# First-layer operands as float16 pairs instead of float32r pairs in a fused attention and two-layer kernel

## The chip, the core and the metric

The kernel runs on one core of a Trainium2 chip. The metric is the device time of one execution in microseconds (us). A core has a matrix engine (TensorE, called PE in the profile, with its weight loads as PEld), a vector engine (DVE), an activation engine (ACT), a general engine (POOL) and a queue engine (SP) that issues transfers. Each takes its own instructions in program order.

## The reference

Three stages follow one another; all tensors are float32 except the four weight matrices of the layers, which come as float64.

```python
kv_pool = kv.reshape(B, H // 4, 4, W // 4, 4, C).mean(axis=(2, 4))   # 384 x 32 -> 96 x 8 = 768 keys, C = 128
k = v = kv_pool.reshape(B, -1, C) @ w_sr
s = (q @ k.transpose(0, 2, 1)) / np.sqrt(C)                          # 12288 queries
a = np.exp(s - s.max(-1, keepdims=True)); a /= a.sum(-1, keepdims=True) + 1e-09
x = a @ v
h = x @ moe_w_in                                                     # 128 -> 2048
x2 = (h * np.clip(h + 3.0, 0.0, 6.0) / 6.0) @ moe_w_out              # 2048 -> 128
h2 = x2 @ moe2_w_in
g = np.where(h2 >= 1, h2, np.where(h2 <= -1, 0.0, (h2 + 1) ** 2 / 4))
out = g @ moe2_w_out
```

## The kernel before

A product of two float32 matrices is made of parts. Each operand is split into a high part and a low part (the remainder), and three matmuls are summed in PSUM: high by high, high by low, low by high. In attention's second product the parts are float16; everywhere else (queries and keys, both layers) they are float32r, a 32-bit type of the matrix engine.

The 12288 queries are 24 blocks of 512. The hidden width of 2048 is 8 pairs of 128-wide pieces, so a block has 8 **slots**, 192 in all. In slot T the function `slot` (L589) issues, for layer 1: `m_in` (L458 on: 6 matmuls of 512 columns into two PSUM tiles `h`), `relu1` on ACT, `mul1` on DVE, `hi_lo` (ACT makes the high part, POOL subtracts to get the low part) and, a slot later, `m_out` (L467: 6 matmuls of 512 columns that add to `acc`). Layer 2 runs 11 slots behind layer 1 in the same slots, with `clip2` and `max2` on DVE and `sq2` on ACT in place of relu and product. Four PSUM tiles `h` go round: two for layer 1 and two for layer 2. So a slot has 24 matmuls of 512 columns, 12 of each layer. Layer 2 alone is left in the last 11 slots.

The attention of later blocks is spread over the slots: in a block of slots there are four score steps (`s_mm`: 6 float32r matmuls of 384 columns, a maximum on DVE, an exponential on ACT), four tails (`s_tail_a`, `s_tail_b`: L423 and L428 on DVE, then a transposing DMA) and two value steps (`av`: 18 float16 matmuls of 256 columns, then L448 on ACT and L449 on DVE, which scale and split `x`).

Ahead of the slots a hand-written order, the string PROLOGUE, gives every step of the start: pooling of the 12 key loads (`k`, `g`, `t`), keys and values (`p`, `z`, `y`), scores and softmax of block 0 (`s`, `S`, `n`, `N`, `e`, `a`, `b`), the scale of V (`vm`, `vr`, `vs`), its parts (`vh`, `vl`), the two value products of block 0 (`x0`, `x1`), and parts of the weight conversion. `j5.1` is stage 1 of weight job 5. There are 16 weight jobs (a quarter of one matrix each, 512 KB of float64), and every job has four stages: two ACT instructions (stage 0), two on DVE and one on POOL (stage 1), one on DVE (stage 2), and a high and a low part (stage 3). What the prologue doesn't do is done in the slots that CONV_AT lists. The string LOADS gives the order of loads; a load is issued when a staging buffer is free. Staging buffers are borrowed from the tiles of the slots (`t1`, `h1`, `l1`, `g2`, `h2`, `l2`, two each) and two of their own (`wst`).

## Time and profile before

| what | value |
|---|---|
| median of 3 runs | 1358.77 us (1357.54 to 1359.09) |
| the profiled execution | 1357.68 us |
| its span, first to last instruction | 1355.9 us |
| PE busy | 1316.6 us, 97% |
| PEld busy | 1074.1 us, 79% |
| DVE busy | 1160.5 us, 86% |
| POOL busy | 1072.3 us, 79% |
| ACT busy | 1035.9 us, 76% |
| mean granted TensorE clock | 0.990 of full speed |

Busy shares are means over the whole span. Matmuls overlap in the records, so the time of one matmul in a stream is read from the distance between starts and not from its own length. An engine is the limit of a stretch where it has no idle time there and the others have.

### The profile page before, as it was taken

What the parts mean: (1) busy time and instruction counts of PE and PEld (TensorE: products, weight loads), DVE (VectorE), ACT (ScalarE), POOL (GpSimd) and SP (SyncE); (2) the same over time, 40 slices, a digit from 0 to 9 for tenths busy, and PEclk for the clock granted to TensorE, in tenths of its full rate; (3) what the DMA queues carried; (4) which work ended last, traced back from release to release, by engine and by line L of the source; (5) the groups of instructions that cost most, each with busy time, mean ns of one, the idle gap of its engine ahead of it and who ended that gap; (6) DMA issues with size and microseconds to landing.
All of it is one profiled execution on the core that took longest, in us unless ns stands there. A gap on an engine that the chain in (4) does not pass through costs nothing.

```text
span 1355.9 us, 18468 instructions
## 1 busy us (share of the span) xinstructions
PE 1316.6 (97%) x6247; PEld 1074.1 (79%) x6247; DVE 1160.5 (86%) x1817; ACT 1035.9 (76%) x1917; POOL 1072.3 (79%) x825
## 2 busy tenths in 40 slices
PE   8578999999999999999999999999999999999998
PEld 7466788888888888888888888888888888888876
DVE  3888978888998988988889989889888889898677
ACT  3777888877777777787778777777877787777776
POOL 2488998888887887887888878878878888787886
PEclk9788999999999999999999999999999999999999
DMA  9632121221221212221212212222222122121001
GB/s 327 156 66 59 39 52 36 39 51 31 44 41 35 51 32 44 40 44 31 51 32 43 44 31 52 32 43 40 44 35 48 32 43 38 30 44 24 8 9 16
DMA packets 260783, 66.28 MB, mean 49 GB/s; under 512 B 252368, under 2 KB 256592, under 8 KB 260688
## 3 DMA queue, kind: packets, MB, share of 16 engines
q1 hardware_dynamic: 259456, 62.94, 24.0%
q10 hardware_dynamic: 1232, 2.16, 0.4%
q8 instruction: 49, 0.80, 0.2%
q14 instruction: 46, 0.38, 0.1%
HBM read 21.04 MB, written 6.29 MB: 20 GB/s over the span
## 4 chain that ended last, share of the span: by engine, by line
PE 87%; DVE 4%; ACT 1%; POOL 1%; issue 1%; DMA 0%; ACTq 0%; DVEq 0%; POOLq 0%
PE acc L480 38%; PE h L464 37%; PE s L371 6%; PE s L443 6%; POOL l L540 1%; DVE t L511 1%; DVE a L428 1%; DVE wa L173 0%; DVE nm L382 0%; ACT t L505 0%; DVE wa L175 0%; DMA wst<-in_moe_w_out_dram 0%; ACT a L421 0%; DVE g L518 0%; ACT h L539 0%
## 5 line engine op out<-in xcount | busy, mean ns | idle before, releaser
L540 POOL TENSOR_TENSOR l<-g,h 128x512 fp32r<-128x512 f32 x382 | 507.0, 1349 | 222.6 <-ACT h L539 175.2
L540 POOL TENSOR_TENSOR l<-t,h 128x512 fp32r<-128x512 f32 x382 | 496.0, 1321 | 9.6 <-ACT h L539 7.2
L505 ACT ACTIVATE t<-h 128x512 f32<-128x512 f32 x384 | 228.2, 599 | 219.1 <-PE h L464 202.7
L511 DVE SCALAR_TENSOR_TENSOR t<-t,h 128x512 f32<-128x512 f32 x384 | 249.7, 683 | 129.4 <-ACT t L505 129.3
L528 DVE TENSOR_TENSOR g<-h,g 128x512 f32<-128x512 f32 x384 | 245.9, 682 | 13.5 <-ACT g L524 6.7
L539 ACT CAST h<-t 128x512 fp32r<-128x512 f32 x384 | 225.2, 620 | 34.9 <-DVE t L511 29.6
L518 DVE TENSOR_SCALAR g<-h 128x512 f32<-128x512 f32 x384 | 246.1, 682 | 1.1 <-POOL l L540 0.6
L524 ACT ACTIVATE g<-g 128x512 f32<-128x512 f32 x384 | 228.2, 629 | 1.9 <-DVE g L518 1.9
L539 ACT CAST h<-g 128x512 fp32r<-128x512 f32 x384 | 217.6, 617 | 4.3 <-DVE g L528 4.0
L464 PE MATMUL h<-xh,wi0h 128*128 128x512 f32 x384 | 153.5, 400 | 4.1 <-ACT xh L448 2.7
L480 PE MATMUL acc<-h,wo0h 128*128 128x512 f32 x384 | 157.1, 409 | 0.0
L480 PE MATMUL acc<-l,wo0h 128*128 128x512 f32 x384 | 154.7, 403 | 2.1 <-POOL l L540 2.0
L464 PE MATMUL h<-x2h,wi1h 128*128 128x512 f32 x384 | 152.8, 398 | 2.4 <-DVE g L528 2.2
L480 PE MATMUL acc<-h,wo0l 128*128 128x512 f32 x384 | 153.2, 399 | 0.0
L464 PE MATMUL h<-xh,wi0l 128*128 128x512 f32 x384 | 152.8, 398 | 0.0
L480 PE MATMUL acc<-h,wo1l 128*128 128x512 f32 x384 | 152.8, 398 | 0.0
L464 PE MATMUL h<-xl,wi0h 128*128 128x512 f32 x384 | 152.6, 398 | 0.0
L464 PE MATMUL h<-x2l,wi1h 128*128 128x512 f32 x384 | 152.6, 397 | 0.0
L480 PE MATMUL acc<-h,wo1h 128*128 128x512 f32 x384 | 152.0, 396 | 0.5 <-DVE o L496 0.4
L480 PE MATMUL acc<-l,wo1h 128*128 128x512 f32 x384 | 152.1, 396 | 0.0
L464 PE MATMUL h<-x2h,wi1l 128*128 128x512 f32 x384 | 151.6, 395 | 0.0
L428 DVE SCALAR_TENSOR_TENSOR a<-e,rc,a 128x768 f16<-128x768 f32 x96 | 122.7, 1278 | 2.8
(139 smaller groups left out, 2142.6 us busy)
## 6 DMA issues: line engine op xcount, KB each, us to landing
q<-in_q_dram SPq DMA_DIRECT2D x96, 64.0 KB, 2.4
out_dram<-o SPq DMA_DIRECT2D x96, 64.0 KB, 2.0
h<-in_kv_dram SPq DMA_DIRECT2D x4, 512.0 KB, 9.5
l<-in_moe_w_in_dram SPq DMA_DIRECT2D x3, 512.0 KB, 8.7
at<-a SPq DMA_TRANSPOSE x96, 3.6
...
```

Of the source, the lines that this page charges most:

```text
L371: nc.tensor.matmul(ps[h], l[:, js], r[:, ks], start=(n == 0), stop=(n == 2))
L428: nc.vector.scalar_tensor_tensor(out=a[:, 1], in0=e, scalar=rc, in1=a[:, 0], op0=ALU.mult, op1=ALU.subtract)
L443: nc.tensor.matmul(ps, l[:, k, :], r[:, k, :], start=(n == 0), stop=(n == 3 * KC - 1))
L464: nc.tensor.matmul(ps, l[:, ws], r, start=(n == 0), stop=(n == 2))
L480: nc.tensor.matmul(acc[m], l[:, ws], r[:, k, :], start=(c == 0 and i == 0), stop=(c == NPAIR - 1 and i == 5))
L505: nc.scalar.activation(out=g_t[0, s][:, k], in_=h_t[0, s, k], func=ACTF.Relu, scale=1.0 / 6.0, bias=0.5)
L511: nc.vector.scalar_tensor_tensor(out=g, in0=g, scalar=1.0, in1=h_t.pop((0, s, k)), op0=ALU.min, op1=ALU.mult)
L518: nc.vector.tensor_scalar(out=g_t[1, s][:, k], in0=h_t[1, s, k], scalar1=1.0, scalar2=-1.0, op0=ALU.min, op1=ALU.max)
L524: nc.scalar.activation(out=g, in_=g, func=ACTF.Square, scale=0.5, bias=0.5)
L528: nc.vector.tensor_tensor(out=g, in0=h_t.pop((1, s, k)), in1=g, op=ALU.max)
L539: nc.scalar.copy(out=hi[:, k], in_=g[:, k])
L540: eng.tensor_tensor(out=lo[:, k], in0=g[:, k], in1=f32(hi[:, k]), op=ALU.subtract)
```

## The change

The layer-1 operands (`x`, the matrices `moe_w_in` and `moe_w_out`, and the activations between them) get float16 parts. Float16 has a narrow range, so they are scaled: `x` stays in units of V's power-of-two scale, and each weight matrix is multiplied by a factor taken from its largest magnitude; `relu1`, `mul1` and the step that makes `x2` take the factors back out, with the per-partition scalars `h_sc` and `o_sc` (`relu1` had a constant before). The largest magnitude needs all four quarters of a matrix before the first of them is converted: 8 new steps `m0` to `m7` (a maximum over a quarter, on DVE), two chains `ia ib ic` and `oa ob oc` (maximum, PE transpose, nine small DVE instructions on one partition, PE broadcast, one DVE product) and `hs`. Loads and prologue steps are put in another order, the staging pool `wst` gets 6 buffers in place of 2, and `h1`, `l1` (now half as large) no longer serve as staging nor, in the last 11 slots, as buffers of layer 2.

```diff
-LOADS = "w k0 k1 w k4 k6 k2 k5 k3 w q0 k8 k7 k9 k10 k11 w w w w w q1 w w w w w w q2 w w"
+LOADS = "w k0 k1 w w w k4 k6 k2 k5 k3 q0 k8 k7 k9 k10 k11 w w w w q1 w w w w w q2 w w w"
-j0.0 j0.1 k0 j1.0 k1 j0.2 k2 k3 g2 k4 g3 j1.1 t1 k5 j2.0 j0.3 p1 q0 k6 z1 t2 j2.1 p2 t0
-j1.2 j1.3 k7 j2.2 p0 z0 k8 t3 z2 k9 p3 s0 y3 k10 z3 y2 k11 n0 t4 y1 s2 t5 p4 p5
-n2 j3.0 z4 z5 y5 s1 y4 n1 j4.0 y0 S2 S0 j3.1 N0 j2.3 S1 N1 s3 n3 N2 e0 e1 vm S3
-a0 j3.2 vr b0 e2 a1 j4.1 N3 e3 a2 b1 vs a3 vh b2 b3 vl j5.0 j3.3 j5.1 q1 j4.2 j5.2 j6.0 x0
-j4.3 x1 j6.1 j5.3
+m0 k0 m2 k1 m4 k2 m6 ia k3 g2 ib k4 ic g3 j0.0 j2.0 t1 k5 j0.1 p1 q0 k6 z1 t2 j2.1 p2 t0
+j0.2 j4.0 k7 j0.3 j2.2 p0 z0 k8 t3 z2 k9 j2.3 j4.1 p3 s0 y3 k10 z3 y2 k11 n0 t4 y1 s2 t5 p4 p5
+n2 j4.2 z4 z5 y5 s1 y4 n1 m1 y0 S2 S0 m3 N0 j4.3 m5 S1 N1 m7 oa s3 n3 N2 e0 ob e1 vm S3
+a0 oc vr j1.0 b0 e2 a1 j1.1 N3 e3 a2 b1 j3.0 vs a3 vh b2 b3 vl hs j1.2 j3.1 q1 j1.3 j3.2 j5.0 x0
+j3.3 x1 j5.1
+N_ST = 6
+W_DT = (FP16, F32R)
+H_SC = 2.0 ** -22
-CONV_AT = (0, 1, 4, 6, 7, 8, 10, 12, 14)
+CONV_AT = (0, 1, 4, 6, 7, 8, 10, 12, 13, 14)
-    w_in = [[const.tile([128, DFF], F32R, name=f"wi{m}{p}") for p in "hl"] for m in range(2)]
+    w_in = [[const.tile([128, DFF], W_DT[m], name=f"wi{m}{p}") for p in "hl"] for m in range(2)]
...
-        tags = (("t1", "h1", "l1", "g2", "h2", "l2"), ("g2", "h2", "l2"), ("wst",))[late]
+        tags = (("t1", "g2", "h2", "l2", "wst"), ("g2", "h2", "l2", "wst"), ("wst",))[late]
...
+    def w_max(job):
+        m, which, i = job
+        n = 2 * m + (which == "out")
+        nc.vector.tensor_reduce(out=mw[n][:, i:i + 1], in_=wst[job][0][:, :, 1].bitcast(FP32),
+                                axis=AX.X, op=ALU.max, apply_absolute_value=True)
+    def w_top(n, ps):
+        nc.vector.tensor_reduce(out=mw[n][:, 0:1], in_=mw[n], axis=AX.X, op=ALU.max)
+        nc.tensor.transpose(ps[0:1, :], mw[n][:, 0:1], ident)
+    def w_row(n, ps, bc):
+        nc.vector.tensor_reduce(out=top[:, 4:5], in_=ps[0:1, :], axis=AX.X, op=ALU.max)
...
+        nc.tensor.matmul(bc, ones, top[:, 0:4])
+    def w_scales(n, bc):
+        nc.vector.tensor_tensor(out=w_sc[n], in0=bc, in1=w_k, op=ALU.mult)
...
-            x_t[b] = [x_p.tile([128, BLK], F32R, tag=f"x{p}", name=f"x{p}") for p in "hl"]
+            x_t[b] = [x_p.tile([128, BLK], FP16, tag=f"x{p}", name=f"x{p}") for p in "hl"]
...
-            out=g_t[0, s][:, k], in_=h_t[0, s, k], func=ACTF.Relu, scale=1.0 / 6.0, bias=0.5
+            out=g_t[0, s][:, k], in_=h_t[0, s, k], func=ACTF.Relu, scale=h_sc, bias=0.5 * H_SC
-            out=g, in0=g, scalar=1.0, in1=h_t.pop((0, s, k)), op0=ALU.min, op1=ALU.mult
+            out=g, in0=g, scalar=H_SC, in1=h_t.pop((0, s, k)), op0=ALU.min, op1=ALU.mult
...
-        n = 1 if m == 0 or (s >= NS - O2 and s % 2) else 2
-        hi = hl_p.tile([128, 2, 512], F32R, tag=f"h{n}", name=f"h{n}")
-        lo = hl_p.tile([128, 2, 512], F32R, tag=f"l{n}", name=f"l{n}")
+        n = m + 1
+        dt = W_DT[m]
+        hi = hl_p.tile([128, 2, 512], dt, tag=f"h{n}", name=f"h{n}")
+        lo = hl_p.tile([128, 2, 512], dt, tag=f"l{n}", name=f"l{n}")
...
+    load_order = [0, 2, 4, 6, 1, 3, 5, 7] + list(range(8, 16))
```

## Rows read from the trace of the kernel before

**Rows 1.** Busy time of each engine by stage of the span, granted clock behind it.
```profile
0.00:56.50 56.50, 37.40 (x259) 31.43 (x259) 31.57 (x71) 26.60 (x59) 18.13 (x19) 0.88 0.87 257
56.50:170.00 113.50, 99.05 (x440) 76.80 (x441) 103.39 (x149) 92.81 (x170) 96.79 (x67) 0.94 0.31 66
170.00:1315.00 1145.00, 1144.58 (x5401) 937.86 (x5400) 992.54 (x1547) 888.60 (x1643) 929.08 (x718) 1.00 0.22 38
```
**Rows 2.** The chain that ended last, shares of the span by line.
```profile
PE acc L480 38%; PE h L464 37%; PE s L371 6%; PE s L443 6%; POOL l L540 1%; DVE t L511 1%; DVE a L428 1%; DVE wa L173 0%; DVE nm L382 0%; ACT t L505 0%; DVE wa L175 0%; DMA wst<-in_moe_w_out_dram 0%; ACT a L421 0%; DVE g L518 0%; ACT h L539 0%
```
**Rows 3.** Timeline of PE: first and last matmul of three unbroken runs.
```profile
696.37 0.39 PE L443 MATMUL s<-at,vh 128*128 128x256 f16 x2
698.23 0.27 PE L443 MATMUL s<-at,vl 128*128 128x256 f16 x1
...
701.15 0.40 PE L464 MATMUL h<-xh,wi0h 128*128 128x512 f32 x1
703.73 0.39 PE L464 MATMUL h<-x2h,wi1l 128*128 128x512 f32 x1
703.96 0.34 PE L371 MATMUL s<-kTh,qh 128*128 128x384 f32 x1
704.84 0.34 PE L371 MATMUL s<-kTh,ql 128*128 128x384 f32 x1
```
**Rows 4.** One block of eight slots: PE, PEld, DVE, ACT, POOL busy.
```profile
595.60:648.74 53.14, 53.14 (x254) 43.62 (x253) 46.99 (x73) 41.14 (x76) 42.61 (x33) 1.00 0.22 40
```
**Rows 5.** The same stretch as the second of rows 1, ACT's `relu1` alone.
```profile
56.50:170.00 113.50, 19.84 (x36) 0.94 0.31 66
```
**Rows 6.** Timeline of PE and DVE in that block, around its tightest place.
```profile
596.46 1.33 DVE L511 SCALAR_TENSOR_TENSOR t<-t,h 128x512 f32<-128x512 f32 x2 [2.32 <-ACT t L505]
603.22 1.93 DVE L428 SCALAR_TENSOR_TENSOR a<-e,rc,a 128x768 f16<-128x768 f32 x1
607.65 1.29 DVE L528 TENSOR_TENSOR g<-h,g 128x512 f32<-128x512 f32 x2
608.57 0.39 PE L464 MATMUL h<-x2h,wi1h 128*128 128x512 f32 x1
```
**Rows 7.** Groups of ACT that read PSUM, by shape.
```profile
L448 ACT ACTIVATE xh<-s,csc 128x256 fp32r<-128x256 f32 x43 | 19.7, 458 | 0.0
L487 ACT CAST x2h<-acc 128x512 fp32r<-128x512 f32 x24 | 13.8, 576 | 0.0
L278 ACT ACTIVATE kTh<-h 128x128 fp32r<-128x128 f32 x6 | 1.6, 280 | 0.2 <-PE h L272 0.2
```
**Rows 8.** POOL groups: layer 1's subtraction and the conversion's addition; busy, mean ns, idle before.
```profile
L540 POOL TENSOR_TENSOR l<-t,h 128x512 fp32r<-128x512 f32 x382 | 496.0, 1321 | 9.6 <-ACT h L539 7.2 <-issue 2.4
L177 POOL TENSOR_TENSOR wa<-wa,wr 128x512 int32<-128x512 int32 x16 | 21.5, 1347 | 32.7 <-DVE wa L175 31.5 <-DVE su L415 1.2
```
**Rows 9.** Groups of DVE: maxima over 384 and 768 columns.
```profile
L382 DVE TENSOR_REDUCE nm<-s 128x1 f32<-128x768 f32 x94 | 89.7, 955 | 0.3 <-PE s L371 0.3
L376 DVE TENSOR_REDUCE n<-h 128x1 f32<-128x384 f32 x4 | 2.2, 550 | 2.3 <-PE h L371 2.3
```
**Rows 10.** Timeline of the start: PE, then DVE.
```profile
13.99 2.78 PE L246 MATMUL h<-h,pool_m 128*32 128x128 f32 x16
49.38 0.58 PE L443 MATMUL h<-at,vh 128*128 128x256 f16 x2 [8.13 <-DMA at<-a]
...
43.71 1.18 DVE L428 SCALAR_TENSOR_TENSOR a<-e,rc,a 128x768 f16<-128x768 f32 x1
44.81 0.15 DVE L303 TENSOR_SCALAR mxa<-acc 128x1 f32<-128x1 f32 x1
44.99 0.15 DVE L304 TENSOR_SCALAR mxa<-mxa 128x1 uint32<-128x1 uint32 x1
```
**Rows 11.** Timeline of the end: PE and ACT in one slot of layer 2.
```profile
1327.41 0.40 PE L480 MATMUL acc<-h,wo1l 128*128 128x512 f32 x1
1328.17 1.16 ACT L539 CAST h<-g 128x512 fp32r<-128x512 f32 x2 [0.21 <-DVE g L528]
```

More of the change, by code (lines that the diff above doesn't have):

```diff
@@ L154, in w_load @@
         return True
+    mw = [const.tile([128, 4], FP32, name=f"mw{n}") for n in range(4)]
+    wm = {}
+    def w_max(job):
[6 more added lines that the diff above has]
+        nc.tensor.transpose(ps[0:1, :], mw[n][:, 0:1], ident)
@@ L160, in w_stage0 @@
+    def w_scales(n, bc):
+        nc.vector.tensor_tensor(out=w_sc[n], in0=bc, in1=w_k, op=ALU.mult)
     def w_stage0(job):
         t = wst[job][0]
+        m, which, i = job
+        half = W_DT[m] == FP16
+        sc = w_sc[2 * m + (which == "out")]
         a = wk_p.tile([128, WP], U32, tag="wa", name="wa")
         r = wk_p.tile([128, WP], I32, tag="wr", name="wr")
-        nc.scalar.activation(out=a.bitcast(FP32), in_=t[:, :, 1].bitcast(FP32), func=ACTF.Abs)
+        nc.scalar.activation(out=a.bitcast(FP32), in_=t[:, :, 1].bitcast(FP32), func=ACTF.Abs,
+                             scale=sc[:, 0:1] if half else 1.0)
@@ L165, in w_stage0 @@
         low = t.rearrange("p a b -> p (a b)").bitcast(U8).rearrange("p (a b) -> p a b", b=8)
-        nc.scalar.activation(
-            out=r, in_=low[:, :, 3], func=ACTF.Copy, scale=1.0 / 32.0, bias=1.0 / 64.0
-        )
+        if half:
+            nc.scalar.activation(out=r.bitcast(FP32), in_=low[:, :, 3], func=ACTF.Identity,
+                                 scale=sc[:, 2:3], bias=sc[:, 1:2])
+        else:
+            nc.scalar.activation(
+                out=r, in_=low[:, :, 3], func=ACTF.Copy, scale=1.0 / 32.0, bias=1.0 / 64.0
+            )
@@ L181, in w_stage2 @@
         hi32 = wst[job][0][:, :, 1]
-        nc.vector.scalar_tensor_tensor(out=hi32, in0=hi32, scalar=0xC0000000, in1=a,
+        keep = 0x80000000 if W_DT[job[0]] == FP16 else 0xC0000000
+        nc.vector.scalar_tensor_tensor(out=hi32, in0=hi32, scalar=keep, in1=a,
                                        op0=ALU.bitwise_and, op1=ALU.bitwise_or)
@@ L194, in w_stage3 @@
         eng = nc.vector if job in LO_DVE else nc.gpsimd
[L195 removed]
+        h = hi[:, sl] if W_DT[m] == FP16 else f32(hi[:, sl])
+        eng.tensor_tensor(out=lo[:, sl], in0=w, in1=h, op=ALU.subtract)
     def conv_stage(n, st):
@@ L668, in tile_attn_moe_moe2 @@
                 steps[f"j{n}.{st}"] = lambda n=n, st=st: conv_stage(n, st)
+        for n in range(8):
+            steps[f"m{n}"] = lambda n=n: w_max(w_jobs[n])
+        for n, k in enumerate("io"):
+            steps[k + "a"] = lambda n=n: w_top(n, row)
+            steps[k + "b"] = lambda n=n: w_row(n, row, bc[n])
+            steps[k + "c"] = lambda n=n: w_scales(n, bc[n])
         for j in range(4):
```

73 lines of the change are left out of this document (53 added, 20 removed).

## The prediction, made before the changed kernel was run

> **What bounds the kernel now.** I read the busy times by stage first. From 170 to 1315 us PE is busy for 1144.58 of 1145.00 us, while DVE, POOL and ACT have 13 to 22% of that stretch idle [rows 1]. The chain of waits says the same: 75% of the span is two PE lines, the first and second products of the layers (L464, L480), and another 12% attention's products [rows 2]. So in the middle a shorter matmul is a shorter kernel, until another engine takes over. Before 170 us it is otherwise: the first 56.5 us are the start, and of the next 113.5 us PE is idle for 14.5 us, in which DVE (103.39 us busy), POOL and ACT set the pace [rows 1].
>
> Second, the timeline, for what a matmul costs. Starts, not lengths, count. Twelve float32r matmuls of 512 columns go from 701.15 to 703.73 in 11 steps: 0.2345 us each. Six of 384 columns take 5 steps of 0.176. Eighteen float16 ones of 256 columns take 17 steps of 0.1094 [rows 3]. Per column that is 0.458 ns, 0.458 ns and 0.427 ns. The granted clock is 1.00 there [rows 1], and a column at 2.4 GHz is 0.417 ns. So a float32r column costs the same extra at both widths, 10%, which looks like a rate; what the float16 matmul has above its columns is 2.7 ns if it is a fixed part, or 2.6% if it is a rate. The three kinds follow one another without a gap, so a change of type between neighbours costs nothing visible.
>
> Third, one block of eight slots: 53.14 us, all PE; DVE 46.99, POOL 42.61, ACT 41.14 [rows 4]. DVE is the next bound, at 88%.
>
> **The matmuls.** Layer 1 has 12 matmuls of 512 columns in each of 192 slots: 2304. In float16 one takes 0.2160 us (fixed part: 213.3 + 2.7 ns) to 0.2188 us (rate: twice 0.1094) [rows 3]; I take 0.2165, nearer to the fixed part, because the granted clock leaves little else. The saving is 18.0 ns each, 41.4 us in all, between 36.2 and 42.6. A block would fall to 53.14 - 96 x 0.018 = 51.4 us, still above DVE's 46.99 [rows 4].
>
> The Trainium skill (TensorE: Matmul & The Clock Gate, "Back-to-back issue gap") gives the warm distance as N/2.4 plus about 2.5 ns, with no dependence on type; that would be 215.8 ns for 512 columns. The float32r rows do not follow it, they are 18.7 ns above; the float16 rows do within 0.3 ns. By it the saving would be an estimated 43.1 us, and my sum would end 1.7 us lower.
>
> **Where the saving does not arrive: the first slots.** ACT has 36 `relu1` before 170 us, so 18 slots lie in the stretch that DVE, POOL and ACT pace [rows 5]. They hold 18 x 12 x 0.018 = 3.9 us of the saving. PE waits there in some slots only; I give back 2.0, between 0 and 3.9.
>
> **Where it does not arrive: a tight place in each block.** In the block at 595.60 DVE works without a pause from 596.46 on, through a whole tail. The second product of layer 2 in the block's third slot starts at 608.57, and the `max2` that frees its PSUM tile runs as a pair of 1.29 us from 607.65, so its first half ends near 608.30: 0.27 us to spare [rows 6]. Thirty layer-1 matmuls stand on PE from the block's first product to this place, which makes PE 0.54 us earlier; DVE's run begins after three of them, so it starts only 0.05 us earlier and takes as long as before. So 0.27 - 0.54 + 0.05 = -0.22: PE waits 0.22 us once a block. To this comes the new scalar of `relu1`, on which DVE's run begins. An ACT instruction from PSUM takes 280 ns for 128 columns and 576 for 512 with a constant scale, so some 380 for 256; with a per-partition scale it takes 458 [rows 7]: 0.08 us more, if the whole difference is the scalar (0 if it is not). That makes 0.30 us; in 22 blocks 6.6 us. Both ends: nothing, if a tail's L428, 1.93 us here [rows 6], takes the 1.18 us that it has at 43.71 with POOL idle more of the time [rows 10]; 22 us, if the moved POOL work lengthens it by another 0.7 us. ACT itself gets 16 x 0.08 = 1.3 us a block and stays at 42.4 of 51.4 [rows 4].
>
> **POOL's subtraction.** It now reads a float32 and a float16 tile and writes float16. No row has POOL with float16; with float32 it takes 1321 ns and the conversion's integer addition 1347 [rows 8], so I take no change. The lower bound is half of it, which would help nothing that bounds; the upper end is the third rival.
>
> **The start.** It gains eight maxima over 512 columns. Over 384 and 768 columns they take 550 and 955 ns [rows 9]; I take 0.68 us. Four of them and the chain `ia ib ic` come among the key loads. The pooling of `k4`, at 13.99 now, stands on PE behind the broadcast of `ib` [rows 10], which waits for `m6`, that is for four weight quarters that are now loaded ahead of `k4`, then for a transpose and nine small dependent DVE instructions, 0.19 us apart (44.81 to 44.99 [rows 10]), 1.7 us. PE pools almost without a pause after it, so what it loses stays: I take 2.5 us, between 0 (the loads come as early as before) and 4.5 (chain of some 3 us and one more quarter). In the scores of block 0, the other four maxima (2.7 us), the chain's DVE part (2.0) and `hs` (three small instructions, 0.5, behind the path) stand on DVE ahead of `b1`; three conversion pieces leave the stretch and two come in, 0.85 less. `b1` ends at 44.9 and its transposed tile is what the first value product waits for at 49.38 [rows 10]. About 0.4 us falls into DVE's gaps: 3.5 us later, between 0.5 and 5.5. One more weight job is left to the slots, with two POOL instructions of 1.3 us and four of DVE; in the paced stretch I count 1.5 us, between 0 (six own staging buffers also end a wait for a load) and 3.
>
> **The end.** Layer 2 loses its second pair of buffers in the last 11 slots. ACT's high part at 1328.17 overwrites a tile that was read last by a product that started at 1327.41 or before, so it would find it free already [rows 11]. Later slots run one slot more behind, where the wait is real but ends ahead of the next use: 0.5 us, between 0 and 2.
>
> **Sum.** -41.4 + 2.0 + 6.6 + 2.5 + 3.5 + 1.5 + 0.5 = -24.8 on the profiled execution's own 1357.7: 1332.9. That execution is 1.1 below the median of the runs shown, so in terms of the median 1334.0.
>
> **Rivals.** *The gain arrives nearly whole* (chance 0.18). The tight place gives way because DVE's L428 is quicker when POOL moves, and the start costs 3 us: -42 + 1 + 3 = 1320. For it: DVE has 6 us of a block idle [rows 4]. Against it: the idle time is not where the tight place is.
>
> *DVE becomes a second bound* (0.13). Each block loses 1 us rather than 0.30, and the start all of its upper bounds, 11 us: -40 + 3 + 22 + 11 + 1 = 1355. For it: DVE would be at 91% of a block and its L428 doubles beside POOL. Against: only one place of a block has under half a microsecond to spare.
>
> *Slower: POOL is slower with float16* (0.06). A block has 16 subtractions of layer 1 among 42.61 us of POOL [rows 4]. It passes DVE's and PE's new pace when one takes 1321 + (51.4 - 42.6) / 16 = 1.87 us, and the kernel is slower than before from (53.1 - 42.6) / 16 more, 1.98 us, on, before the start is counted. At twice the time, 2.64 us, a block takes 63.7: 23 x 10.6 + 10 = 1601 us. For it: no row shows the type on POOL. Against: integer and float take alike there [rows 8], as if elements were counted. The Trainium skill (GPSIMD Engine Reference, "Elementwise — side-by-side cycle accounting") counts two-input work by elements, 2.6 cycles for each, and not by bytes; by that this rival falls away, but no row here has the type.
>
> *No gain: the extra 21 ns of a float32r matmul belong to long products and not to the type* (0.03). Then only the costs are left: 1357.7 + 2 + 6 = 1366. Against: 384 and 512 columns cost the same per column, and 256 less [rows 3].
>
> **How the numbers follow.** The forecast has 0.60. Its own range, from the bounds taken singly, is 1325 to 1345. The range reaches to the first and into the second rival: 1319 to 1352. Left out are about a third of the first rival, 0.06, two fifths of the second, 0.05, and the last two, 0.09: 0.20. A measurement of this kernel tells about 0.2%, 2.7 us, from no change. Faster than that: forecast, first rival and nearly all of the second, 0.90. Within: 0.02, the edge of the second. Slower: most of the last two, 0.08.
>
> **What would show it.** Right: layer-1 matmuls 0.216 to 0.219 us apart, layer 2 unchanged at 0.2345; a block of about 51.7 us with one PE wait of some 0.3 us for `max2` (L528's line); the first product of layer 1 near 62.5 us in place of 56.56; `relu1` some 0.08 us longer; POOL's layer-1 subtraction at 1.3 us. Wrong: a cadence that stays, PE waits for POOL in every slot, several DVE waits in a block, or a start that costs over 10 us.

## The result, and the profile after

The changed kernel takes 1343.12 us (median of 4, 1342.1 to 1343.68), the kernel before on the same chip 1358.22 us (median of 4, 1357.54 to 1359.09): a ratio of 0.9888 with a 95% interval of 0.987 to 0.9905. The forecast was 1334.0 us, its range 1319 to 1352. So the kernel is faster, as forecast, but by 15.1 us (1.1%) and not by 24.8. The profiled execution has a span of 1341.9 us, 14.0 less than the 1355.9 of before.

Where the 14.0 come from is read best from one event that every slot has: the start of its first `relu1` in the trace. This table is made from those starts (us), for all kernels of this study; the experiments follow below (e10 and e13 are experiment 10, e12 is 11, e14 is 9, the others have their number).

```
                     slot 0  slot 3  slot 9  slot 16  slot 18  slot 191     end
before                 57.8    75.4   110.0    156.4    170.7    1310.3  1355.9
after                  69.8    87.0   121.0    168.2    190.0    1295.3  1341.9
e1_job14_early         70.0    87.3   123.6    168.9    183.1    1288.6  1335.1
e2_ib_before_k3        68.7    86.0   120.0    167.2    189.0    1294.4  1340.9
e3_chain_no_wait       63.2    80.5   114.4    161.7    183.0    1288.3  1334.8
e4_const_scales        60.5    77.8   111.7    158.9    180.4    1286.0  1332.5
e5_const_old_order     63.4    81.0   114.9    160.3    174.6    1279.5  1326.5
e6_const_relu_scale    68.3    85.2   118.8    165.7    186.5    1290.0  1336.5
e7_all_moves           64.2    81.4   117.9    163.2    177.5    1283.0  1329.5
e10_chain_and_jobs     63.9    81.2   115.1    164.1    178.4    1283.5  1330.3
e13_jobs_9_10_12       64.7    82.0   115.9    163.7    178.0    1283.3  1329.8
e12_const_and_jobs     59.4    76.6   110.6    159.5    173.8    1279.2  1326.0
e14_before_plain       57.4    70.3    95.7    135.2    149.5    1289.1  1334.7
e8_plain_slot_jobs     67.0    82.0   107.5    145.9    159.5    1264.6  1311.1
```

The second row less the first, column by column: the start costs 12.0 us, the first 16 slots gain 0.2, slots 16 to 18 lose 7.5, slots 18 to 191 gain 34.3, and the end loses 1.0.

**The long middle.** Busy time by stage, after (the stretches are those of [rows 1], moved to the new events; columns as there):

```profile
0.00:68.70 68.70, 42.16 (x266) 34.77 (x267) 35.94 (x105) 27.01 (x56) 15.64 (x18) 0.88 0.81 231
68.70:189.00 120.30, 93.78 (x438) 54.34 (x437) 107.52 (x152) 97.19 (x171) 97.59 (x72) 0.94 0.28 54
189.00:1301.00 1112.00, 1111.19 (x5407) 729.63 (x5406) 969.02 (x1547) 897.51 (x1643) 876.15 (x714) 1.00 0.23 39
```

PE still fills the third stretch, so what a matmul saves there is saved. The second has become longer with less of PE in it: DVE is busy for 89% of it, PE for 78%. In the chain that ended last, the two product lines, now L553 and L537, have 70% in place of 75% [rows 2], and DVE lines have come in:

```profile
PE acc L553 35%; PE h L537 35%; PE s L516 6%; PE s L444 6%; DVE g L593 1%; DVE t L586 1%; DVE g L603 1%; POOL l L616 0%; DVE wa L236 0%; ACT t L580 0%; ACT h L614 0%; DVE a L501 0%; DVE nm L455 0%; DVE wst L246 0%; ACT g L599 0%
```

The cadence, from the timeline of PE (to hold against [rows 3]):

```profile
687.82 0.39 PE L553 MATMUL acc<-h,wo0h 128*128 128x512 f16 x1
688.05 0.38 PE L553 MATMUL acc<-l,wo0h 128*128 128x512 f16 x1
...
688.91 0.38 PE L553 MATMUL acc<-h,wo0l 128*128 128x512 f16 x1
688.94 0.58 PE L553 MATMUL acc<-h,wo1h 128*128 128x512 f32 x1
689.36 0.39 PE L553 MATMUL acc<-l,wo1h 128*128 128x512 f32 x1
...
690.52 0.39 PE L537 MATMUL h<-xh,wi0h 128*128 128x512 f16 x1
```

From 688.05 to 688.91 four float16 steps take 0.86 us, 0.215 each. The first float32r matmul has a record that begins 0.03 us after the last float16 one, which looks like an overlap; the start of the second one is the sound mark, and 689.36 to 690.52 is 1.16 us for five steps, 0.232 each. So layer 2's cadence is as before within the reading, and the change of type costs nothing. The Trainium skill (TensorE: Matmul & The Clock Gate, "Back-to-back issue gap") gives N/2.4 plus 2.5 ns for the gap of single matmuls at the higher clock, without regard to type, an estimated 215.8 ns for 512 columns: the float16 rows agree, the float32r rows still do not.

One block of eight slots, to hold against the 53.14 us of [rows 4], with DVE, ACT and POOL all short of it:

```profile
590.50:642.06 51.56, 51.56 (x254) 33.98 (x253) 45.75 (x74) 41.50 (x77) 40.34 (x34) 1.00 0.23 42
```

**The groups that the prediction spoke of** ([rows 5, 7, 8, 9]): first ACT's `relu1` before and after and `xh`, then POOL's two subtractions, then one of DVE's new maxima.

```profile
L505 ACT ACTIVATE t<-h 128x512 f32<-128x512 f32 x384 | 228.2, 599 | 219.1 <-PE h L464 202.7 <-POOL l L540 7.0
...
L580 ACT ACTIVATE t<-h,h_sc 128x512 f32<-128x512 f32 x384 | 244.3, 687 | 175.6 <-PE h L537 170.5 <-POOL l L616 5.1
...
L521 ACT ACTIVATE xh<-s 128x256 f16<-128x256 f32 x43 | 15.7, 366 | 2.3 <-PE s L516 2.3
```
```profile
L616 POOL TENSOR_TENSOR l<-g,h 128x512 fp32r<-128x512 f32 x382 | 502.0, 1335 | 243.6 <-ACT h L614 118.5 <-issue 88.3 <-POOL l L616 22.4
L616 POOL TENSOR_TENSOR l<-t,h 128x512 f16<-128x512 f32 x382 | 446.2, 1190 | 12.4 <-ACT h L614 12.4
```
```profile
L178 DVE TENSOR_REDUCE mw<-g 128x1 f32<-128x512 f32 x2 | 1.4, 680 | 3.2 <-DMA g<-in_moe_w_in_dram 3.2
```

`relu1` takes 687 ns, before it took 599. `xh`, whose scale became a constant, falls from 458 to 366. POOL's subtraction is quicker in float16, 1190 ns against 1321; layer 2's, still in float32r, takes 1335 in the same kernel.

**The start**, PE and then DVE, to hold against [rows 10]; the last fence is DVE's pair of low key parts (the remainders of the split keys) in the kernel before:

```profile
15.69 0.37 PE L183 MATMUL acc<-ident,mw 128*1 128x128 f32 x1 [1.68 <-DVE mw L182]
...
20.46 0.58 PE L206 MATMUL acc<-wtop,ones 1*128 1x4 f32 x2 [3.71 <-DVE wtop L204]
20.98 2.77 PE L311 MATMUL h<-t,pool_m 128*32 128x128 f32 x16
...
24.67 2.78 PE L311 MATMUL h<-wst,pool_m 128*32 128x128 f32 x16
...
28.53 1.85 PE L311 MATMUL h<-t,pool_m 128*32 128x128 f32 x16
...
31.64 1.53 PE L311 MATMUL h<-wst,pool_m 128*32 128x128 f32 x16
...
61.64 0.59 PE L516 MATMUL h<-at,vh 128*128 128x256 f16 x2 [9.51 <-DMA at<-a]
```
```profile
17.88 0.69 DVE L303 TENSOR_TENSOR wst<-wst 128x512 f32<-128x512 f32 x1 [2.34 <-DMA wst<-in_kv_dram]
18.60 0.42 DVE L304 TENSOR_TENSOR wst<-wst 128x256 f32<-128x256 f32 x1
18.95 0.27 DVE L190 TENSOR_REDUCE wtop<-acc 1x1 f32<-1x128 f32 x1
...
42.44 0.48 DVE L344 SCALAR_TENSOR_TENSOR kTl<-h,kTh 128x128 fp32r<-128x128 f32 x2
...
55.87 1.21 DVE L501 SCALAR_TENSOR_TENSOR a<-e,rc,a 128x768 f16<-128x768 f32 x1
```
```profile
33.88 0.49 DVE L279 SCALAR_TENSOR_TENSOR kTl<-h,kTh 128x128 fp32r<-128x128 f32 x2 [1.14 <-ACT kTh L278]
```

The pooling of `k4` starts at 20.98 in place of 13.99 [rows 10]. PE stood for 3.71 us at the broadcast; its input came from the small DVE chain from 18.95 on, and DVE stood at 17.88, 2.34 us, for the transfer of `k3`: an add that is issued ahead of the chain and has nothing to do with it. The last pair of low key parts starts at 42.44; before it started at 33.88. That is 8.6 us. From there to `b1` it takes 13.43 us, in place of 9.83 before (33.88 to the 43.71 of [rows 10]): 3.6 more. The first value product, at 61.64, follows, 12.3 later than the 49.38 of [rows 10].

The poolings themselves change their pace: 16 matmuls take 2.77 and 2.78 us at 20.98 and 24.67, and 1.53 from 31.64 on. The trace's record of the granted clock points to why. Its first entry is a rise to 1.00 at 29.2 us (17.0 in the kernel before); ahead of its first entry it says nothing, and the views print 1.00 there all the same. In all fourteen traces of this study the poolings of this form (into 128 columns) go at 0.157 us from matmul to matmul ahead of the first entry and at 0.084 or less behind it. So the long poolings were, as far as this can show it, at the lower level, 1.2 GHz. The rise comes at 24.5 to 29.7 us in the five kernels in which PE stands at the chain (this one and experiments 1, 2, 6 and 8 below), at 16.5 to 23.8 in the nine others. It is not fixed by the program alone: experiments 6 and 8 have the same start as the changed kernel, with nearly the same waits at the chain, and there it came at 24.7 and 24.5 us, and the low key parts started at 40.51 and 40.19. Some 2 of the 8.6 us are thus of this execution and not of the change.

**Slots 16 to 18.** PE, then what it waited for on ACT and POOL:

```profile
177.81 0.50 PE L537 MATMUL h<-x2h,wi1h 128*128 128x512 f32 x1 [2.77 <-ACT wi1h L257]
...
180.80 0.80 PE L537 MATMUL h<-x2h,wi1l 128*128 128x512 f32 x1 [2.26 <-POOL wi1l L260]
```
```profile
177.11 0.64 ACT L257 CAST wi1h<-wst 128x512 fp32r<-128x512 f32 x1
```
```profile
179.45 1.29 POOL L260 TENSOR_TENSOR wi1l<-wst,wi1h 128x512 fp32r<-128x512 f32 x1
```
```profile
180.80:186.20 5.40, 5.40 (x21) 3.70 (x22) 3.98 (x5) 2.84 (x6) 5.14 (x4) 0.50 0.00 0
```

Layer 2 wants the last quarter of its first matrix in slot 17, and that quarter (weight job 14) is cut into its parts only then. PE stands twice, 5.0 us. Behind that the granted clock is 0.50 for 5.4 us (last fence, a row of busy times as above), which is the lower of the two levels, 1.2 GHz.

### The profile page after: what moved, and what is told of

It reads as the page before. It is cut to its first block, busy times and chain, and to the rows that moved or that the text cites. A ratio compares the mean times of both kernels' runs of the same rounds, so it can differ in the third digit from the quotient of the medians.

```text
span 1341.9 us, 18502 instructions
## 1 busy us (share of the span) xinstructions
PE 1281.9 (96%) x6253; PEld 844.7 (63%) x6253; DVE 1144.8 (85%) x1853; ACT 1049.4 (78%) x1917; POOL 1017.4 (76%) x825
## 3 DMA queue, kind: packets, MB, share of 16 engines
q1 hardware_dynamic: 259456, 62.94, 24.8%
## 4 chain that ended last, share of the span: by engine, by line
PE 83%; DVE 5%; ACT 2%; POOL 1%; issue 1%; POOLq 0%; ACTq 0%; DVEq 0%
PE acc L553 35%; PE h L537 35%; PE s L516 6%; PE s L444 6%; DVE g L593 1%; DVE t L586 1%; DVE g L603 1%; POOL l L616 0%; DVE wa L236 0%; ACT t L580 0%; ACT h L614 0%; DVE a L501 0%; DVE nm L455 0%; DVE wst L246 0%; ACT g L599 0%
## 5 line engine op out<-in xcount | busy, mean ns | idle before, releaser
L616 POOL TENSOR_TENSOR l<-g,h 128x512 fp32r<-128x512 f32 x382 | 502.0, 1335 | 243.6 <-ACT h L614 118.5
L616 POOL TENSOR_TENSOR l<-t,h 128x512 f16<-128x512 f32 x382 | 446.2, 1190 | 12.4 <-ACT h L614 12.4
L580 ACT ACTIVATE t<-h,h_sc 128x512 f32<-128x512 f32 x384 | 244.3, 687 | 175.6 <-PE h L537 170.5
L614 ACT CAST h<-t 128x512 f16<-128x512 f32 x384 | 224.8, 619 | 37.0 <-DVE t L586 36.2
L537 PE MATMUL h<-x2h,wi1h 128*128 128x512 f32 x384 | 183.9, 479 | 7.1 <-DVE g L603 3.9
L553 PE MATMUL acc<-h,wo1h 128*128 128x512 f32 x384 | 185.1, 482 | 0.7 <-DVE o L571 0.6
L537 PE MATMUL h<-x2h,wi1l 128*128 128x512 f32 x384 | 152.2, 396 | 2.3 <-POOL wi1l L260 2.3
L537 PE MATMUL h<-xh,wi0h 128*128 128x512 f16 x384 | 148.3, 386 | 5.6 <-ACT xh L521 3.1
L553 PE MATMUL acc<-l,wo1h 128*128 128x512 f32 x384 | 151.4, 395 | 0.7 <-POOL l L616 0.7
L537 PE MATMUL h<-x2l,wi1h 128*128 128x512 f32 x384 | 151.9, 396 | 0.0
L553 PE MATMUL acc<-h,wo1l 128*128 128x512 f32 x384 | 151.5, 394 | 0.0
L553 PE MATMUL acc<-h,wo0h 128*128 128x512 f16 x384 | 147.4, 384 | 1.7 <-DVE su L488 1.7
L553 PE MATMUL acc<-l,wo0h 128*128 128x512 f16 x384 | 146.0, 380 | 2.2 <-POOL l L616 2.1
L537 PE MATMUL h<-xl,wi0h 128*128 128x512 f16 x384 | 146.3, 381 | 0.2
L537 PE MATMUL h<-xh,wi0l 128*128 128x512 f16 x384 | 146.4, 381 | 0.0
L553 PE MATMUL acc<-h,wo0l 128*128 128x512 f16 x384 | 146.1, 380 | 0.0
L537 PEld LDWEIGHTS <-wi0h 128*128 128x128 f16 x768 | 61.2, 98 | 103.8 <-issue 56.6
```

The lines of the kernel that those rows point to most:

```text
L537: nc.tensor.matmul(ps, l[:, ws], r, start=(n == 0), stop=(n == 2))
L553: nc.tensor.matmul(acc[m], l[:, ws], r[:, k, :], start=(c == 0 and i == 0), stop=(c == NPAIR - 1 and i == 5))
L580: nc.scalar.activation(out=g_t[0, s][:, k], in_=h_t[0, s, k], func=ACTF.Relu, scale=h_sc, bias=0.5 * H_SC)
L614: nc.scalar.copy(out=hi[:, k], in_=g[:, k])
L616: eng.tensor_tensor(out=lo[:, k], in0=g[:, k], in1=h, op=ALU.subtract)
```

## The experiments

From these views my theory had three parts: the start is late because TensorE and VectorE stand still behind the scale chain; slots 16 to 18 are late because of job 14; the first 16 slots gain nothing because DVE, with the weight jobs, sets the pace there. The expectations count slot 0 from its first matmul, at 68.7 us in the changed kernel, the table (and the expectation of experiment 7) from its first `relu1`, 69.8; of the last low key parts they give the start (42.4, 41.3) or, for experiment 4, the end (35.8). Rivals: the order of loads sets the start; a weight job costs its instructions wherever it stands; latency from layer to layer sets the pace of the first slots.

**1. Job 14 earlier.**

```diff
-CONV_AT = (0, 1, 4, 6, 7, 8, 10, 12, 13, 14)
+CONV_AT = (0, 1, 3, 4, 6, 7, 8, 10, 12, 14)
```

> The changed kernel with one list altered: the last weight job of the slots (moe2_w_in's last quarter) starts one slot earlier, at slot 12 in place of 13, and the two jobs after slots 1 and 2 move with it. The changed kernel took 1343.1 us. Theory A (TensorE stands still at 178 to 181 us because that quarter is not yet cut into its two parts when slot 17 wants it): the waits of 2.8 and 2.3 us there go, the jump of 7.5 us between slots 16 and 18 shrinks to under 2 us, and the time falls to 1335 to 1338 us. Theory B (one more weight job in the first slots costs what its ScalarE and GpSimd instructions cost, wherever it stands): the jump only moves to other slots, and the time stays within 1341 to 1345 us.

1336.38 us (1334.76 to 1337.05), ratio to before 0.9823 (0.9794 to 0.9852). Theory A. In the same place PE now has one short wait left, for another engine:

```profile
175.82 0.50 PE L537 MATMUL h<-x2h,wi1h 128*128 128x512 f32 x1 [0.40 <-DVE g L603]
```

From slot 16 to 18 it takes 14.2 us (after: 21.8; before: 14.3). The list moves more than job 14: jobs 8 to 13 start one or two slots earlier too. Experiment 10, which moves two jobs only, loses the jump as well. One detail was not expected: at slot 9 the kernel is 2.6 us behind the changed one (53.6 us from slot 0 to 9 in place of 51.2; experiment 7, which has a job at slot 3 too, takes 53.7); by slot 16 all but 0.7 of this is gone.

**2. The chain ahead of the add that waits.**

```diff
-m0 k0 m2 k1 m4 k2 m6 ia k3 g2 ib k4 ic g3
+m0 k0 m2 k1 m4 k2 m6 ia ib ic k3 g2 k4 g3
```

> The changed kernel with the order of its prologue altered: the two later steps of the first-layer scale's chain (the maximum over the transposed row, and the broadcast) are issued right behind the transpose, ahead of the third key pool's add and of the fourth group's pooling, in place of behind them. The changed kernel took 1343.1 us, and its last key transpose ended at 42.4 us, 8.5 us later than before the change. Theory A (VectorE stands behind an add that waits for its transfer while the chain waits, and TensorE behind the chain): the broadcast comes 2 to 3 us earlier, the key phase ends near 40 us, the time is 1340 to 1341 us. Theory B (the key phase is late because V and the weights are loaded ahead of keys): no change in the key phase, 1342.5 to 1344 us.

1341.71 us (1339.79 to 1342.67). PE's timeline:

```profile
18.13 0.58 PE L206 MATMUL acc<-wtop,ones 1*128 1x4 f32 x2 [1.56 <-DVE wtop L204]
18.65 1.06 PE L325 MATMUL h<-pool_m,wst 128*128 128x32 f32 x4
19.64 2.78 PE L311 MATMUL h<-t,pool_m 128*32 128x128 f32 x16
```

The broadcast comes 2.33 us earlier, so the add did hold it up. Only 1.16 us reaches the keys (last low parts from 41.28), as another pooling now stands ahead of `k4`'s, and the time lies between the two theories. PE still waits at the transpose and at the broadcast.

**3. The chain threaded between the poolings.**

```diff
-m0 k0 m2 k1 m4 k2 m6 ia k3 g2 ib k4 ic g3
+m0 k0 m2 k1 m4 k2 m6 g2 ia k4 ib k3 ic g3
```

> The changed kernel with the first scale chain threaded between the key poolings, so that TensorE and VectorE always have ready work ahead of each of its steps: the transposed maximum stands behind the second group's pooling, the row maximum ahead of the add that waits for a transfer, the broadcast behind the fourth add group's pooling. Nothing is left out. The changed kernel took 1343.1 us and its last key transpose ended at 42.4 us; with constant scales it ended at 35.8 us, with the chain merely ahead of the add at 41.3 us. Theory A (it is the standing still behind the chain, and the half clock granted after it, that cost the key phase): the last key part is done by 36 to 38.5 us, the time is 1337 to 1339.5 us. Theory B (VectorE's work for four maxima and a chain of ten small instructions, some 4.5 us, is itself the price): key phase at 40 us or later, 1341 to 1343.5 us.

1337.71 us (1336.66 to 1339.08), ratio 0.985 (0.9836 to 0.9865). Theory A: the last low key parts start at 36.43, 6.0 us earlier, with the same maxima and the same chain. PE's timeline (the transpose, `k4`, the broadcast and the next two poolings):

```profile
15.51 0.40 PE L183 MATMUL acc<-ident,mw 128*1 128x128 f32 x1
15.84 2.69 PE L311 MATMUL h<-t,pool_m 128*32 128x128 f32 x16
18.46 0.38 PE L206 MATMUL acc<-wtop,ones 1*128 1x4 f32 x2
18.86 0.63 PE L325 MATMUL h<-pool_m,wst 128*128 128x32 f32 x4
19.43 1.53 PE L311 MATMUL h<-wst,pool_m 128*32 128x128 f32 x16
```

No step of the chain waits on PE any more. Part of the gain is seen in the lengths: a pooling of 16 matmuls takes 1.53 us from 19.43 on, where in the changed kernel those at 20.98 and 24.67 take 2.77 and 2.78 and the one at 28.53 takes 1.85. Those three poolings are worth 2.8 us (each against 1.53). Here the record of the granted clock begins with its rise at 18.3 us, in the changed kernel at 29.2. How much of that is due to the order and how much to the execution stays open: in the four kernels with this order (3, 7 and both of 10) the low key parts start between 36.43 and 37.71, in the four with the start of the changed kernel (it, 1, 6 and 8) between 40.19 and 42.47. So order is worth 2.5 to 6.0 us there, 4.3 on the mean.

**4. Constant scales: no maxima, no chains.**

```diff
-m0 k0 m2 k1 m4 k2 m6 ia k3 g2 ib k4 ic g3 j0.0
+k0 k1 k2 k3 g2 k4 g3 j0.0
...
-y4 n1 m1 y0 S2 S0 m3 N0 j4.3 m5 S1 N1 m7 oa s3 n3 N2 e0 ob e1 vm S3
-a0 oc vr
+y4 n1 y0 S2 S0 N0 j4.3 S1 N1 s3 n3 N2 e0 e1 vm S3
+a0 vr
...
+                nc.gpsimd.memset(w_sc[n][:, c:c + 1], v)
```

> The changed kernel without its scale steps: the maxima of the weights' magnitudes and both chains from them to the scale tiles are left out, and constants of the same values are written into the tiles; loads, order of conversions and everything else stay as changed. The changed kernel took 1343.1 us, its start stands 11.9 us behind that of the kernel before (first slot at 68.7 against 56.6 us). Theory A (the scale steps themselves hold up VectorE and TensorE in the key phase): the first slot starts at 60 to 63 us and the time is 1335 to 1338 us. Theory B (the new order of loads and of weight jobs delays the keys, whatever is computed from them): the first slot stays at 66 us or later, and the time at 1341 us or more.

1333.98 us (1333.46 to 1335.38), ratio 0.9809 (0.978 to 0.9837). Theory A, with a little more than it allowed: slot 0 is 9.3 us earlier. The low key parts end their run from 35.28 on (7.2 us earlier) and `b1` follows 10.3 us later (in place of 13.4). So of the start's 12.0 us the scale steps account for 9.3 in these executions, 9.1 by the medians. The other 2.7 belong to what is left of the change at the start (order of loads and steps, staging buffers, scaled conversions), which this run does not take apart.

**5. The same with the old order of loads, prologue and jobs.** On top of 4, LOADS, PROLOGUE (with `hs` added), CONV_AT and `load_order` as before the change; the staging pool keeps its 6 buffers.

```diff
-LOADS = "w k0 k1 w w w k4 k6 k2 k5 k3 q0 k8 k7 k9 k10 k11 w w w w q1 w w w w w q2 w w w"
+LOADS = "w k0 k1 w k4 k6 k2 k5 k3 w q0 k8 k7 k9 k10 k11 w w w w w q1 w w w w w w q2 w w"
...
-    load_order = [0, 2, 4, 6, 1, 3, 5, 7] + list(range(8, 16))
+    load_order = list(range(16))
```

> As the kernel with constant scales (maxima of the magnitudes and both chains left out), and besides with the loads, the order of the prologue and the slots of the weight jobs as in the kernel before the change. What is left of the change is float16 parts, scaled conversions and the per-partition scale of the first activation. Theory A (the start's whole loss comes from scale steps and order): first slot at 56.5 to 58 us, no jump at slots 16 to 18, the rest falls by 0.2 us per slot from the first slot on, and the time is 1319 to 1325 us. Theory B (the first 17 slots are bound by the weight conversions on ScalarE and GpSimd, which float16 does not make shorter): first slot at 57 us, no gain until slot 17, 1323 to 1327 us. Theory C (scaled conversions hold up the start by themselves): first slot at 61 us or later, over 1328 us.

1328.5 us (1328.19 to 1333.88), ratio 0.978 (0.974 to 0.9819). The numbers are those of theory C, but slot 0 starts at 63.4, later than in 4, though the scaled conversions are the same; that they hold up the start is not shown. Part of what is different stands in SP's queue, here and, in the second fence, before the change, with the DVE instruction that ends the first tail ahead of it:

```profile
36.77 8.23 SPq L410 DMA_DIRECT2D q<-in_q_dram  x4
45.05 1.08 SPq L159 DMA_DIRECT2D wst<-in_moe_w_in_dram  x1
46.24 0.38 SPq L162 DMA_DIRECT2D wst<-in_moe_w_out_dram  x1
46.72 9.98 SPq L507 DMA_TRANSPOSE at<-a  x4
```
```profile
40.56 1.00 DVE L428 SCALAR_TENSOR_TENSOR a<-e,rc,a 128x768 f16<-128x768 f32 x1
...
41.58 8.38 SPq L434 DMA_TRANSPOSE at<-a  x4
```

The transposes of block 0 start at 46.72 in place of 41.58: 5.1 of the 5.6 us by which slot 0 is late. Two causes share this. Before, they start as the first tail ends, at 41.6; here that tail ends at 43.96, 2.4 later, and the transposes start another 2.75 later, behind weight loads and a load of queries that before the change came after them. The 2.4 begin in the key phase: the low key parts start at 36.03 in place of 33.88. PE has no wait in either kernel from 6.2 us until past the pooling of `k4` at 14.0, and the next pooling takes 2.78 us here and 1.53 before; the clock's rise is recorded at 21.6 and at 17.0. The 2.75 are the queue's. That six staging buffers let the loads go earlier, and that the new order of LOADS pays for it, fits 4, where the transposes start 0.5 us behind the tail; no run changes the number of buffers alone, so it is argued. What 5 shows besides: with the old slots for the jobs there is no jump (14.3 us from slot 16 to 18), and the first 16 slots gain 1.7 us (96.9 against 98.6).

**6. A constant scale in `relu1`.**

```diff
-            ..., func=ACTF.Relu, scale=h_sc, bias=0.5 * H_SC
+            ..., func=ACTF.Relu, scale=2.0 ** -25 * H_SC / 6.0, bias=0.5 * H_SC
```

> The changed kernel with the scale of the first activation given as a constant of the instruction in place of a pointer to a value per partition (the value depends on the data and so is left out of the computation). In the changed kernel one such activation takes 0.69 us on the mean, 0.60 before. Theory A (TensorE waits once per block at the tight place because this activation is longer): the activation falls to 0.60 us, a block to 51.4 us or less, and the time by 1 to 3 us, to 1340 to 1342 us. Theory B (the wait there comes from shorter matmuls meeting VectorE and GpSimd, whose work is as long as before): activation 0.60 us, time within 1342.5 to 1344 us.

1339.79 us (1338.29 to 1340.31). `relu1` falls from 687 to 597 ns:

```profile
L580 ACT ACTIVATE t<-h 128x512 f32<-128x512 f32 x264 | 154.7, 597 | 142.2 <-PE h L537 140.6 <-POOL l L616 1.6
```

What PE's weight loads wait for DVE's `max2` between 300 and 1150 us, some 16 blocks, the changed kernel first and this one second:

```profile
PEld h L537 <- DVE g L603: 7.0, 17, 0.7
```
```profile
PEld h L537 <- DVE g L603: 5.5, 17, 0.5
```

Theory A has the sign right and the smaller part of the size. From slot 18 to slot 191 this kernel takes 1103.5 us, the changed one 1105.3: 1.8 us, some 0.08 a block, is what the pointer costs. All eleven kernels with the pointer and the float16 parts take 1104.9 to 1105.6 there, so this is clear of the noise. The wait stays, one per block; the kernel before has none for `max2` in that window. So most of it comes from shorter matmuls, as theory B has it. The rest of the 3.3 us that the medians differ by lies ahead of slot 18; in the profiled execution 1.5 us lie ahead of slot 0, in steps that this edit does not touch, where the clock rose at 24.7 us in place of 29.2.

**7. Both moves together, and the second chain spread out.** Experiments 1 and 3 in one, and the maxima `m1 m3` ahead of `n2`, `m5` behind `z5`, `oa` behind the last scores, `ob` behind `S3`.

```diff
-n2 j4.2 z4 z5 y5 s1 y4 n1 m1 y0 S2 S0 m3 N0 j4.3 m5 S1 N1 m7 oa s3 n3 N2 e0 ob e1 vm S3
+m1 m3 n2 j4.2 z4 z5 m5 y5 s1 y4 n1 y0 S2 S0 N0 j4.3 S1 N1 m7 s3 n3 N2 oa e0 e1 S3 ob vm
```

> All moves together, nothing left out: the last weight job one slot earlier, the first scale chain threaded between the poolings, and the second chain's four maxima spread into idle stretches of VectorE, with its transpose behind the last scores and its broadcast behind those of the second half. The changed kernel took 1343.1 us; the first move alone took 6.8 us off. If the start's loss is standing still that order can take away, the first slot starts at 62 to 65 us in place of 69.8 and the time is 1328 to 1332 us. If the maxima and chains cost their work wherever they stand, it stays at 1335 to 1336.5 us.

1331.46 us (1331.1 to 1336.76), ratio 0.9813 (0.9793 to 0.9832). As hoped for the two moves. The third brought nothing: from the low key parts (37.33) to `b1` (50.58) it takes 13.25 us, in 3 it took 13.42.

**8. Slot jobs without their rounding.** On top of 1, the ten jobs in slots do only the cast and the subtraction; the rounding is left out, so the weights go in unrounded and without their scale factor.

```diff
+        if n in plain and st < 3:
+            conv[n] = st + 1
+            return
```

> The kernel with the last weight job one slot earlier (1336.4 us), and of the ten weight jobs that run in slots only the cast and the subtraction: their rounding (two ScalarE, three VectorE instructions and one GpSimd instruction per job) is left out, so that these weights are used unrounded. Theory A (in the first 17 slots VectorE sets the pace, weight jobs with it, and so shorter matmuls win nothing there): the slots up to 17 fall by 5 to 12 us, the time is 1324 to 1332 us. Theory B (the pace there is the latency from layer to layer with one block in flight, not the load of VectorE): no slot falls by more than 2 us, 1334 to 1337 us.

1313.87 us (1312.74 to 1317.72), 22.5 less than 1. Theory A in the time, and by far more than I had expected: from slot 3 to slot 16 it takes 63.9 us in place of 81.6. In the profiled executions 3.0 us of the difference lie ahead of slot 0, which the edit does not touch (the clock's rise again, at 24.5 us in place of 29.7). As the rounding goes, ACT and POOL lose work together with DVE, so this run does not say which of the three set the pace.

**9. The same in the kernel before the change.**

```diff
+    plain = range(7, 16)
...
+        if n in plain and st < 3:
+            conv[n] = st + 1
+            return
```

> The kernel before the change with the rounding of the nine weight jobs that run in slots left out, so that these weights are used unrounded: the counterpart, in float32r parts, of the changed kernel whose slot jobs have no rounding either. From slot 3 to slot 17 that one took 70.1 us, against 89.4 us with the rounding; the kernel before the change took 87.8 us with it. Theory A (with the rounding VectorE sets the pace and hides the shorter matmuls; without it TensorE sets it): this kernel takes 72 to 74 us from slot 3 to slot 17, 0.15 to 0.25 us a slot more than the float16 one. Theory B (something else in these slots sets the pace, matmuls never): 69.5 to 71 us, as the float16 one.

1337.79 us (1336.44 to 1338.83), ratio 0.985 (0.9834 to 0.9867). From slot 3 to slot 17 it takes 71.6 us, between the two theories. Busy times from 80 to 150 us, in this order: before the change, experiment 1, then without rounding in float32r and in float16.

```profile
80.00:150.00 70.00, 61.44 (x279) 48.37 (x280) 62.73 (x89) 56.66 (x105) 60.72 (x43) 0.93 0.30 59
```
```profile
80.00:150.00 70.00, 51.74 (x244) 29.37 (x242) 64.25 (x92) 57.36 (x102) 56.80 (x42) 0.93 0.36 68
```
```profile
80.00:150.00 70.00, 68.45 (x340) 55.65 (x339) 54.58 (x87) 60.88 (x111) 62.52 (x47) 1.00 0.32 65
```
```profile
80.00:150.00 70.00, 65.15 (x337) 40.70 (x338) 55.66 (x91) 64.27 (x118) 59.91 (x48) 1.00 0.35 70
```

With the rounding, DVE is the busiest engine (62.73 and 64.25 of 70 us) and PE falls to 51.74 as its matmuls shrink: it waits longer. But DVE is not full, and what PE itself waits for is ACT more than DVE (the exponential `e` follows a maximum on DVE). These are PE's three longest waits between 62 and 168 us in the kernel before (us in total, times, longest):

```profile
PE s L371 <- ACT e L407: 6.4, 4, 2.9
PE h L464 <- DVE g L528: 2.2, 1, 2.2
PE h L464 <- ACT xh L448: 2.2, 1, 2.2
```

Without the rounding, DVE falls below PE, PE reaches 68.45 in float32r at a granted clock of 1.00 in place of 0.93, and the float16 kernel gains 1.5 us over 14 slots, about half of the 0.2 us a slot that it gains in the middle, with ACT (64.27) now nearly as busy as PE; it also has ten jobs in slots where this one has nine. So neither theory had the size. The rounding sets the pace of the first slots and hides the shorter matmuls there; without it they show in half. That it does so through DVE rather than ACT is not shown.

**10. Where the jobs should stand.** Experiment 3, with jobs at slots 10, 11, 12, 14 and at 9, 10, 12, 14 in place of 10, 12, 13, 14.

```diff
-CONV_AT = (0, 1, 4, 6, 7, 8, 10, 12, 13, 14)
+CONV_AT = (0, 1, 4, 6, 7, 8, 10, 11, 12, 14)
...
+CONV_AT = (0, 1, 4, 6, 7, 8, 9, 10, 12, 14)
```

> The kernel with the first scale chain threaded between the poolings (1337.7 us) and, besides, the last two weight jobs of the slots one slot earlier each (at slots 11 and 12 in place of 12 and 13), the early ones left where they were; nothing left out. Theory A (the jump at slots 16 to 18 is only that the last quarter comes too late for slot 17; a job moved to slot 3 cost 1 to 2.6 us that this placing avoids): no jump, nothing lost at slots 4 to 9, 1328 to 1330.5 us. Theory B (a job more in these slots costs its VectorE time wherever it stands): the loss returns at slots 11 to 16, 1331 to 1334 us.

> The same with the last four weight jobs at slots 9, 10, 12 and 14 in place of 10, 12, 13 and 14; nothing left out. Theory A: the jump is gone here as well, and the time is within 1 us of the kernel with jobs at 10, 11, 12 and 14, 1328 to 1331 us. Theory B (the place decides little, the load of VectorE all): the same too, but above 1331 us.

1332.09 us (1331.74 to 1337.93) and 1331.62 us (1330.15 to 1332.05). The jump from slot 16 to 18 is gone in both (14.3 us), and part of it is back in the slots ahead: from slot 9 to 16 the first takes 49.0 us, experiment 3 47.3. By their times both fall to theory B, the second by 0.6 us, less than its runs differ by; between the places tried, 7 among them, nothing can be told apart.

**11. What the chains still cost.** The first kernel of 10 with the constant scales of 4.

```diff
-m0 k0 m2 k1 m4 k2 m6 g2 ia k4 ib k3 ic g3 j0.0
+k0 k1 k2 g2 k4 k3 g3 j0.0
...
-y4 n1 m1 y0 S2 S0 m3 N0 j4.3 m5 S1 N1 m7 oa s3 n3 N2 e0 ob e1 vm S3
-a0 oc vr
+y4 n1 y0 S2 S0 N0 j4.3 S1 N1 s3 n3 N2 e0 e1 vm S3
+a0 vr
...
+                nc.gpsimd.memset(w_sc[n][:, c:c + 1], v)
```

> The kernel with jobs at slots 10, 11, 12 and 14, but with constant scales: maxima of the weights' magnitudes and both chains are left out, constants of the same values stand in the tiles. What it is faster than that kernel is what the chains still cost once nothing stands still behind the first. Theory A (the second chain in the scores phase of block 0, four maxima and its small instructions on VectorE, some 3 us): first slot 2.5 to 3.5 us earlier, 1325 to 1327.5 us. Theory B (the second chain is covered by waits that are there anyway): within 1 us of that kernel.

1329.7 us (1327.8 to 1330.31), 2.4 less than 10 by the medians. In the profiled executions slot 0 is 4.5 us earlier, of which 3.1 lie between low key parts and `b1` (10.33 us against 13.4). So the second chain is not covered by waits; how much of both chains reaches the end, between 2.4 and 4.3, the spread of the runs leaves open.

## Why the prediction was right, and where it was off

The mechanism held: PE fills the middle, a float16 matmul is shorter, the saving arrives there and not at the start. The sign came out with it. Of the signs that the prediction named, the cadence, the block, the one wait for `max2` and the longer `relu1` came as said. POOL's subtraction takes 1.19 us and not 1.3, layer 1 did not begin near 62.5 us but at 68.7, and one sign of being wrong came true: the start costs over 10 us, 12.0. The size was off by 9.1 us by the medians (10.8 between the profiled executions), from terms that err in both directions. The start and the job more in the slots missed by 6 us each; that the time still lies inside the forecast's own 1325 to 1345 owes some 4 us to the matmuls and the tight place, which came out better than forecast. That much of it is luck.

- **The matmuls, forecast -41.4.** From 687.82 to 690.52 twelve matmuls, six of each type, take 2.70 us; less 6 x 0.2345 that is 1.293, or 0.2155 for a float16 one. So 0.019 us for each of 2304, -44. The forecast's 0.2165 lay between a fixed part (0.2160) and a rate (0.2188); the fixed part was right.
- **The tight place, forecast 0.30 us a block, 6.6 in all.** It is there, once a block, and the wait is for `max2`, as forecast. A block of the middle takes 51.56; 53.14 less 96 x 0.019 is 51.3, so it loses 0.25. From slot 18 to 191 the saving should be 173 x 12 x 0.019 = 39.4 and is 34.3: 5.1 us. A good term. The pointer's share was forecast at 0.08 and measured so in experiment 6. The Trainium skill (ScalarE: Activation LUTs, "What ACT_TABLE_LOAD costs") gives about 93 ns for each pointer operand; `relu1` has 88 (687 - 599) and `xh` 92 (458 - 366).
- **The first slots, forecast to give back 2.0 of 3.9.** They gave back nearly all of it: 0.2 us gained in 16 slots. The step "PE waits there in some slots only" was wrong: there the waits grow by what the matmuls shrink. Experiments 8 and 9 show what sets the pace, the rounding of the weight jobs; on which engine is not shown.
- **The job more in the slots, forecast 1.5, at most 3.** 7.5 us. I had costed its instructions on POOL and DVE and not asked when its result is wanted. Job 14 ends in the slot that needs it, PE stands for 5.0 us and then runs at half clock; experiments 1 and 10 show it, as with the job earlier the jump is gone, and 1 is 6.7 us faster.
- **The key phase of the start, forecast 2.5, at most 4.5.** 8.6 us, and this is the term that failed most. "For four weight quarters, then for a transpose and nine small instructions" was the right chain, costed at its own length; left out was that `ib` stands on DVE behind an add that waits 2.34 us for the transfer of `k3`, and that the poolings behind such a stop stay long until the clock rises, which is later then. Some 2 us are of the execution, as shown above. Experiment 3 gets 6.0 us back, in the profiled executions; by the medians order alone is worth 5.4 (3 against the changed kernel) and 4.9 (7 against 1).
- **The scores of block 0, forecast 3.5.** Measured 3.6, and experiment 4 puts 3.1 of it to the chain and its maxima.
- **The end, forecast 0.5.** 1.0.

Three figures of the prediction are slips on which nothing hangs. The third rival's sum, 1357.7 + 23 x 10.6 + 10, comes to 1611 and not to 1601. The bounds, taken one at a time, give 1327 to 1349 and not 1325 to 1345. And 44.81 to 44.99 is 0.18 us, not 0.19.

The rivals: POOL is not slower with float16 but 10% faster. That float32r's extra time goes with the length and not with the type is refuted by the cadence. The second bound did not come in the middle. The wide ends of my unknowns for the start were too narrow, since both were built on lengths of instructions and not on order.

Two moves of order (experiment 10; experiment 7 has a third, which brought nothing) make a faster kernel than either: 1331 to 1332 us, 11 to 12 us below the changed kernel and 26 to 27 below the one before.
